# Exponentials in a pair of PSUM banks, scores through one bank by halves, three expert banks, three score copies and one E

## The chip, the cores and the metric

The kernel runs on one core of a Trainium2 chip. The metric is the device time of one execution in microseconds (us). The engines are PE (TensorE matmuls; PEld is its weight load), DVE (VectorE), ACT (ScalarE), POOL (GpSimd) and SP (SyncE, which issues the DMAs). SBUF is the working memory, PSUM the eight banks of 128 x 512 fp32 into which the matmuls write.

## The reference

Attention with a top-32 mask feeds two expert layers, all of it dense.

```python
scores = (1 / sqrt(D)) * q @ k.T                    # B=4, H=8, S=576, D=64
kth = 32nd largest score of each row
attn = softmax(where(scores >= kth, scores, -1e9))
x = (attn @ v) as (B*S, H*D)                        # 2304 tokens x 512
h = x @ w_in                                        # 512 x 2048
g = where(h >= 1, h, where(h <= -1, 0, (h + 1)**2 / 4))
x = g @ w_out                                       # 2048 x 512
out = (silu(x @ w_gate) * (x @ w_val)) @ w_out2     # 512 x 1536, 1536 x 512
```

The weights come as 64-bit floats. The kernel converts each of 68 blocks of 128 x 512 of them into a pair of fp32r tiles (high and low part), and a product is three fp32r passes.

## The kernel before, in words

**Planner.** The program first lists operations (`p.op(engine, planned duration, function, reads, writes, ...)`). A list scheduler (`Plan.schedule`) then lays them out forwards and backwards `ROUNDS` times with planned durations and a ring of buffers for each kind of tile, and keeps the shortest plan. The order in that plan is the program order of every engine, and engines run it strictly in order. A number such as `PORT` (added to the planned time of a conversion step) or `PS` only changes the order.

**Attention.** A unit is one batch b, one pair of heads hp and one block of query tiles: 256 queries (two tiles) or 320 (two and a half). A query tile has two heads (the half tile one), 144 tile-heads in all, 36 for each batch. Batch 0 runs "plain" (fp32 matmuls, lines 767 to 771), the others in fp32r passes (line 775). For each tile-head `qtile` does this: PE writes 128 x 576 scores into `pS`, a pair of PSUM banks (halves of 288 columns); ACT copies them to `C` in SBUF (L792); DVE finds the 32 largest by four rounds of MAX8 (L794) and three of MATCH_REPLACE8 (L804, into `R`); POOL makes the bias `nb` from the maximum (L798); ACT writes exp(scores) into `E` in SBUF (L801); and DVE applies the mask in place, reading `C` and `E` and writing `E` with the row sum (L808). PE then transposes `E` (L852 to L872), ACT takes the result out of the banks `pT` (L832, L837, L839), POOL makes low parts (L841). `outputs` multiplies by V (L696 plain, L707 and L709 otherwise), normalises and stores to `xs` in DRAM.

**Conversions.** `convert` makes one weight block: a DMA into `cv`, two ACT steps (L932, L935), a DVE step (L937), a POOL step (L940), ACT (L942), POOL (L944), and a DMA to scratch. With `bank` the DVE step reads one operand from a `pM` bank; without, both come from SBUF. The first `BANKED` = 24 conversions use a bank. The ten held ones come first, then 28 early ones, then 30 later ones inside the first two expert steps.

**Experts.** 2304 tokens run in groups of 256 (the last of 512) through fourteen steps, layer 1 or 2 of one or two groups each. `proj` (L1060) fills a `pM` bank with 24 matmuls of 256 columns or 12 of 512; layer 1 then takes it out by ACT Relu (L1136), ACT Square (L1138) and DVE min/max (L1140, which reads the bank again); layer 2 by ACT Tanh (L1196) and DVE (L1198, L1208). Second products are L1102 and L1174. There are four `pM` banks. After the attention the banks of `pS` and `pT` become expert banks too (named `late`). The first group's input is block 0 of batch 0, kept in SBUF; the second group's comes from block 1 of batch 0 through `xs`.

PSUM before: `pS` 2, `pT` 2, `pM` 4. SBUF rings that matter: `C` 2, `E` 2, `R` 2.

## Time and profile before

| | us |
|---|---|
| median of 3 runs (1304.3 to 1309.76) | 1307.21 |
| the profiled execution, whole time | 1309.97 |
| its span, first to last instruction | 1308.2 |
| PE busy (94% of the span) | 1225.9 |
| DVE busy (81%) | 1054.9 |
| ACT busy (69%) | 898.6 |
| POOL busy (60%) | 790.0 |

The difference of 1.8 us between the execution and its span lies around the first and last instruction. Busy shares are means over stages: attention lasts until about 1028 us, and after it only expert matmuls are left, so that DVE's 81% is a full engine for four fifths of the time. A matmul is counted busy from its start to its modelled end, so a busy PE has to be held against the pace of its matmuls.

### The profile page before, as it was taken

What the parts mean: (1) busy time and instruction counts of PE and PEld (TensorE: products, weight loads), DVE (VectorE), ACT (ScalarE), POOL (GpSimd) and SP (SyncE); (2) the same over time, 40 slices, a digit from 0 to 9 for tenths busy, and PEclk for the clock granted to TensorE, in tenths of its full rate; (3) what the DMA queues carried; (4) which work ended last, traced back from release to release, by engine and by line L of the source; (5) the groups of instructions that cost most, each with busy time, mean ns of one, the idle gap of its engine ahead of it and who ended that gap; (6) DMA issues with size and microseconds to landing.
All of it is one profiled execution on the core that took longest, in us unless ns stands there. A gap on an engine that the chain in (4) does not pass through costs nothing.

```text
span 1308.2 us, 23150 instructions
## 1 busy us (share of the span) xinstructions
PE 1225.9 (94%) x7744; PEld 1090.6 (83%) x7744; DVE 1054.9 (81%) x2070; ACT 898.6 (69%) x1921; POOL 790.0 (60%) x797
## 2 busy tenths in 40 slices
PE   3566799998999999999999999999999999999998
PEld 2444588886999999999999988889999888888887
DVE  6989999999999999999999999999999512222212
ACT  5767787678897788878989887779786421332220
POOL 4767778698886577857587774667654512213210
PEclk9967699999999999999999999999999999999999
DMA  7987799889998787877875844447768554666452
GB/s 214 346 251 261 264 325 327 323 284 317 350 332 311 255 321 271 300 263 252 321 253 208 307 136 152 148 171 282 288 241 301 194 201 163 231 226 231 154 193 65
DMA packets 145479, 328.16 MB, mean 251 GB/s; under 512 B 33616, under 2 KB 75088, under 8 KB 145360
## 3 DMA queue, kind: packets, MB, share of 16 engines
q1 hardware_dynamic: 145360, 326.69, 71.5%
q8 instruction: 61, 1.00, 0.3%
q14 instruction: 58, 0.48, 0.1%
HBM read 282.07 MB, written 44.56 MB: 250 GB/s over the span
## 4 chain that ended last, share of the span: by engine, by line
PE 68%; DMA 11%; DVE 10%; ACT 4%; issue 3%; POOL 3%; SPq 1%; POOLq 0%; DVEq 0%; ACTq 0%
PE pM L1060 27%; PE pM L1102 9%; PE pM L1174 8%; PE late L1060 5%; PE pS L775 4%; PE pT L707 4%; DVE v L794 4%; DVE R L804 3%; PE pT L852 3%; PE late L1174 2%; PE late L1102 2%; DMA cv<-in_moe_w_out_dram 2%; DMA ws_moe_w_out<-cv 2%; DMA cv<-in_moe_w_in_dram 1%; DVE E L808 1%
## 5 line engine op out<-in xcount | busy, mean ns | idle before, releaser
L794 DVE MAX8 v<-R 128x8 f32<-128x576 f32 x432 | 314.1, 746 | 0.9
L1060 PE MATMUL pM<-w,w 128*128 128x256 f32 (+1 forms) x1734 | 296.9, 314 | 3.2 <-DMA w<-ws_moe_w_in 1.9
L1060 PEld LDWEIGHTS pM<-w,w 128*128 128x128 f32 x1734 | 245.5, 192 | 22.7 <-DMA w<-ws_moe_w_in 2.6
L969 POOL TENSOR_TENSOR w<-t,w 128x512 fp32r<-128x512 f32 x106 | 142.4, 1346 | 189.4 <-ACT w L967 155.7
L841 POOL TENSOR_TENSOR late<-F,late 128x384 fp32r<-128x384 f32 (+1 forms) x180 | 179.4, 1008 | 61.9 <-ACT F L839 53.6
L804 DVE MATCH_REPLACE8 R<-v,R 128x576 f32<-128x576 f32 x288 | 212.6, 739 | 0.0
L808 DVE SCALAR_TENSOR_TENSOR E<-C,v,E 128x576 f32<-128x576 f32 x144 | 157.7, 1095 | 0.1
L1102 PE MATMUL pM<-w,w 128*128 128x256 f32 (+1 forms) x897 | 133.4, 292 | 0.0
L852 PE MATMUL pT<-idf,E 128*128 128x128 f32 x512 | 93.7, 292 | 41.3 <-DVE E L808 35.4
L792 ACT ACTIVATE C<-pS 128x576 f32<-128x576 f32 x144 | 94.0, 653 | 43.8 <-DVE E L808 37.7
L801 ACT ACTIVATE E<-C,nb 128x576 f32<-128x576 f32 x144 | 112.6, 783 | 15.4 <-POOL nb L798 14.7
L1102 PEld LDWEIGHTS pM<-w,w 128*128 128x128 f32 x897 | 117.7, 191 | 3.8 <-issue 1.5
L794 DVE MAX8 v<-C 128x8 f32<-128x576 f32 x144 | 107.4, 746 | 14.8 <-ACT C L792 13.8
L940 POOL TENSOR_TENSOR ct<-ct,cv 128x512 int32<-128x512 int32 x68 | 92.5, 1362 | 43.0 <-DVE cv L937 12.9
L852 PEld LDWEIGHTS pT<-idf,E 128*128 128x128 f32 x512 | 65.1, 148 | 58.1 <-DVE E L808 29.1
L967 ACT ACTIVATE w<-t 128x512 fp32r<-128x512 f32 x106 | 67.1, 635 | 59.2 <-DVE t L1208 52.6
L1060 PE MATMUL pM<-late,w 128*128 128x256 f32 (+1 forms) x618 | 107.4, 309 | 0.0
L804 DVE MATCH_REPLACE8 R<-v,C 128x576 f32<-128x576 f32 x144 | 106.5, 740 | 0.0
L837 ACT ACTIVATE late<-pT 128x384 fp32r<-128x384 f32 (+1 forms) x180 | 84.9, 472 | 14.2 <-PE pT L865 4.7
L1060 PEld LDWEIGHTS pM<-late,w 128*128 128x128 f32 x618 | 86.9, 190 | 4.9 <-POOL late L969 0.2
L1174 PE MATMUL pM<-w,w 128*128 128x512 f32 x324 | 88.8, 405 | 0.7 <-POOL w L944 0.6
L1060 PE MATMUL pM<-w,late 128*128 128x256 f32 (+1 forms) x456 | 86.1, 325 | 0.0
(151 smaller groups left out, 2661.3 us busy)
## 6 DMA issues: line engine op xcount, KB each, us to landing
w<-ws_moe_w_out SPq DMA_DIRECT2D x144, 512.0 KB, 5.9
w<-ws_moe_w_in SPq DMA_DIRECT2D x91, 512.0 KB, 6.3
w<-ws_moe_w_gate SPq DMA_DIRECT2D x56, 512.0 KB, 5.8
w<-ws_moe_w_val SPq DMA_DIRECT2D x51, 512.0 KB, 6.3
late<-ws_moe_w_out SPq DMA_DIRECT2D x40, 512.0 KB, 6.0
cv<-in_moe_w_out_dram SPq DMA_DIRECT2D x28, 512.0 KB, 5.2
late<-ws_moe_w_in SPq DMA_DIRECT2D x27, 512.0 KB, 6.5
cv<-in_moe_w_in_dram SPq DMA_DIRECT2D x16, 512.0 KB, 5.3
```

The lines of the kernel that those rows point to most:

```text
L792: p.op("ACT", self.act(576), lambda sc=sc, cc=cc: nc.scalar.activation(out=cc(), in_=sc(), func=AF.Copy), [ps], [Cb], 1, "scp")
L794: p.op("DVE", self.dve(576), lambda: nc.vector.max(out=v8[:, h, k, :], in_=rr() if k else cc()), [Rb if k else Cb], [(v8, (h, k))], 6, "max8")
L801: p.op("ACT", self.act(576, self.FN), lambda h=h, cc=cc, ee=ee: nc.scalar.activation(out=ee(), in_=cc(), func=AF.Exp, bias=nb[:, h:h + 1], ...
L804: p.op("DVE", self.dve(576) + 0.06, lambda h=h, k=k, cc=cc, rr=rr: nc.vector.match_replace(out=rr(), in_to_replace=v8[:, h, k, :], in_valu ...
L808: p.op("DVE", self.dve(576) + 0.06, lambda h=h, cc=cc, ee=ee: nc.vector.scalar_tensor_tensor(out=ee(), in0=cc(), scalar=v8[:, h, 3, 7:8], ...
L841: p.op("POOL", self.pool(n), lambda: nc.gpsimd.tensor_tensor(out=dst(1), in0=src(F), in1=dst(0).bitcast(F32), op=OP.subtract), [F, (PT, (0 ...
L852: fn = (lambda ps=ps, m=m, h=h, c=c: nc.tensor.transpose(ps[:, m * 128:(m + 1) * 128], Sb[:, h, 64 * h + c * 128:64 * h + (c + 1) * 128], ...
L940: p.op("POOL", self.pool(512), lambda: nc.gpsimd.tensor_tensor(out=ci(), in0=ci(), in1=word(0), op=OP.add), [(cv, 0)], [ct], 3, tag + "cvadd")
L969: p.op("POOL", self.pool(n), lambda: nc.gpsimd.tensor_tensor(out=dst[:, 1, to:to + n], in0=src[:, off:off + n], in1=dst[:, 0, to:to + n].b ...
L1060: nc.tensor.matmul(ps[:, at:at + n], W[:, w, k * 128:(k + 1) * 128], x[:, s, xat:xat + n], start=k == 0 and j == 0, stop=k == KC - 1 and j ...
L1102: nc.tensor.matmul(ps[:, at:at + n], WO[f][:, v, j * 128:(j + 1) * 128], g[:, s, gat:gat + n], start=q == 0 and m == 0, stop=q == 3 and m ...
L1174: nc.tensor.matmul(ps[:], a[:, s, at:at + 128], WO[f][:, v, :], start=q == 0 and m == 0, stop=q == 3 and m == 2)
```

## The change

Exponentials get their own ring `pE` of one pair of PSUM banks; ACT writes them there, and the mask reads them from there and writes `E` in SBUF. To pay for it, `pS` becomes one single bank, through which the two halves of a tile-head's scores pass one after the other, each with its own ACT copy of 288 columns; and `pM` goes from four banks to three. `C` goes from two buffers to three, `E` from two to one. `BANKED` goes to 40, which covers all 28 early conversions (14 of them before). `ROUNDS` goes from 4 to 10 and `PORT` from 0 to .38, which act on the order alone. The four zero fills of `vF` move out of the plan to the program's start.

```diff
-    ROUNDS = 4
+    ROUNDS = 10
...
-    VIA, BANKED = 0, 24
+    VIA, BANKED = 0, 40
...
+    PE_N, PM, PS_N, CN, EN, FB = 1, 3, 1, 3, 1, 2
...
-    SB, FN, PS, PORT = 0.043, 0.136, 0.065, 0.0
+    SB, FN, PS, PORT = 0.043, 0.136, 0.065, 0.38
...
-        self.r_E = R("E", [128, 2, S], F32, 2)
+        self.r_E = R("E", [128, 2, S], F32, self.EN)
...
-        self.p_s = R("pS", [128, 2, 512], F32, 1, "P")
-        self.r_C = R("C", [128, S], F32, 2)
+        self.p_s = R("pS", [128, 512], F32, self.PS_N, "P")
+        self.r_C = R("C", [128, S], F32, self.CN)
+        self.p_e = R("pE", [128, 2, 512], F32, self.PE_N, "P")
         self.p_t = R("pT", [128, 512], F32, self.PT_BANKS, "P")
-        self.p_m = R("pM", [128, 512], F32, 6 - self.PT_BANKS, "P")
+        self.p_m = R("pM", [128, 512], F32, self.PM, "P")
...
-        p.op("DVE", self.dve(1280), lambda: nc.vector.memset(vF[:], 0.0), [], [vF], 1, "vz")
...
-            ps = self.p_s.new()
             Rb = self.r_R.new()
+            Cb = self.r_C.new()
             for j in (0, 1):
+                ps = self.p_s.new()
...
+                p.op("ACT", self.act(288), lambda j=j, ps=ps, Cb=Cb: nc.scalar.activation(
+                    out=Cb[:, j * 288:(j + 1) * 288], in_=ps[:, 0:288], func=AF.Copy), [ps], [(Cb, j)], 1, "scp")
...
-            p.op("ACT", self.act(576), lambda sc=sc, cc=cc: nc.scalar.activation(out=cc(), in_=sc(), func=AF.Copy), [ps], [Cb], 1, "scp")
...
-            p.op("ACT", self.act(576, self.FN), lambda h=h, cc=cc, ee=ee: nc.scalar.activation(
-                out=ee(), in_=cc(), func=AF.Exp, bias=nb[:, h:h + 1], scale=0.125), [Cb, (nb, h)], [(Eb, h)], 1, "exp")
+            Ep = self.p_e.new()
+
+            def ep(Ep=Ep):
+                return Ep[:, :, 0:288]
+            p.op("ACT", self.act(576, self.FN), lambda h=h, cc=cc, ep=ep: nc.scalar.activation(
+                out=ep(), in_=cc(), func=AF.Exp, bias=nb[:, h:h + 1], scale=0.125), [Cb, (nb, h)], [Ep], 1, "exp")
...
-            p.op("DVE", self.dve(576) + 0.06, lambda h=h, cc=cc, ee=ee: nc.vector.scalar_tensor_tensor(
-                out=ee(), in0=cc(), scalar=v8[:, h, 3, 7:8], in1=ee(),
+            p.op("DVE", self.dve(576) + 0.06 + self.PS, lambda h=h, cc=cc, ee=ee, ep=ep: nc.vector.scalar_tensor_tensor(
+                out=ee(), in0=cc(), scalar=v8[:, h, 3, 7:8], in1=ep(),
                 op0=OP.is_ge, op1=OP.mult, accum_out=rs[:, i, h:h + 1]),
-                [Cb, (v8, (h, 3))], [(Eb, h), (rs, (i, h))], 5, "mask")
+                [Cb, Ep, (v8, (h, 3))], [(Eb, h), (rs, (i, h))], 5, "mask")
...
+        for r in self.r_vF:
+            nc.vector.memset(r.slots[0][:], 0.0)
```

What this does to the order is seen at three places. The first is DVE's order before, from the first mask to the second (a name's number tells the buffer: `C_283`, `C_284` are the two copies, `E_232` and `E_233` the two E).

```order
L808 SCALAR_TENSOR_TENSOR E_232,rs_243<-C_283,v_236,E_232 128x576
L937 SCALAR_TENSOR_TENSOR cv_278<-cv_278,pM_289 128x512
L804 MATCH_REPLACE R_235<-v_236,R_235 128x576
L937 SCALAR_TENSOR_TENSOR cv_279<-cv_279,pM_290 128x512
L794 MAX v_237<-C_283 128x8
L794 MAX v_236<-R_235 128x8
L804 MATCH_REPLACE R_234<-v_237,C_283 128x576
L808 SCALAR_TENSOR_TENSOR E_232,rs_243<-C_284,v_236,E_232 128x576
```

And the same stretch of DVE's order now, where line numbers are one to three off.

```order
L809 SCALAR_TENSOR_TENSOR E_232,rs_242<-C_282,v_235,pE_285 128x576
L791 MAX v_235<-R_234 128x8
L791 MAX v_236<-C_284 128x8
L805 MATCH_REPLACE R_234<-v_235,R_234 128x576
L805 MATCH_REPLACE R_233<-v_236,C_284 128x576
L938 SCALAR_TENSOR_TENSOR cv_277<-cv_277,pM_288 128x512
L791 MAX v_235<-R_234 128x8
L938 SCALAR_TENSOR_TENSOR cv_278<-cv_278,pM_289 128x512
L809 SCALAR_TENSOR_TENSOR E_232,rs_242<-C_283,v_235,pE_285 128x576
```

Both masks now read the one pair `pE_285`, so the exponential of the second stands between them; the third tile-head has a copy of its own (`C_284`), while before it had to wait for the first mask to give `C_283` back.

The second place is PE's order where the first expert step begins, before: a tile-head's scores (L769) go into the pair `pS_282` one after the other, and the experts rotate through four banks.

```order
L769 MATMUL pS_282<-kF_220,qF_228 128x64
L769 MATMUL pS_282<-kF_220,qF_228 128x224
L769 MATMUL pS_282<-kF_220,qF_228 128x288
L852 MATMUL pT_285<-idf,E_232 128x128 x2
L852 MATMUL pT_286<-idf,E_232 128x128 x2
L856 MATMUL pT_286<-idf,E_232 128x128
L769 MATMUL pS_282<-kF_220,qF_228 128x288
L1060 MATMUL pM_287<-w_265,w_254 128x256 x6
```

The same place of PE's order now.

```order
L1061 MATMUL pM_288<-w_264,w_253 128x256 x6
L1061 MATMUL pM_288<-w_263,w_255 128x256 x6
L1061 MATMUL pM_288<-w_264,w_255 128x256 x3
L770 MATMUL pS_281<-kF_220,qF_228 128x288
L1061 MATMUL pM_288<-w_264,w_255 128x256 x3
L1061 MATMUL pM_289<-w_264,w_257 128x256 x6
L1061 MATMUL pM_289<-w_263,w_259 128x256 x6
L1061 MATMUL pM_289<-w_264,w_259 128x256 x6
L770 MATMUL pS_281<-kF_221,qF_229 128x288
L1061 MATMUL pM_290<-w_264,w_261 128x256 x6
```

Between two halves of scores, which share `pS_281`, stand 21 expert matmuls, and the experts rotate through `pM_288` to `pM_290`.

The third place is DVE's order now, at the end of batch 1 (three masks near each other).

```order
L809 SCALAR_TENSOR_TENSOR E_232,rs_242<-C_282,v_237,pE_285 128x576
L805 MATCH_REPLACE R_234<-v_235,R_234 128x576
L791 MAX v_235<-R_234 128x8
L809 SCALAR_TENSOR_TENSOR E_232,rs_242<-C_283,v_237,pE_285 128x576
L791 MAX v_236<-C_282 128x8
L821 RECIPROCAL rc_245<-rs_242 128x4
L809 SCALAR_TENSOR_TENSOR E_232,rs_242<-C_284,v_235,pE_285 128x576
```

The last two masks have only a MAX8 and a reciprocal between them, and need the exponential pair and the one `E` in turn.

## Rows read from the trace of the kernel before

**Rows 1.** Four stretches: length, busy us of PE, PEld, DVE, ACT, POOL; clock, DMA share, GB/s.
```profile
0.00:160.00 160.00, 97.09 (x310) 64.83 (x310) 136.71 (x265) 111.10 (x214) 108.85 (x110) 0.80 0.83 269
160.00:331.00 171.00, 160.25 (x1030) 136.86 (x1030) 170.26 (x312) 138.32 (x281) 141.30 (x119) 0.98 0.90 312
331.00:1030.00 699.00, 694.50 (x5188) 661.84 (x5188) 687.43 (x1408) 577.68 (x1306) 475.74 (x519) 1.00 0.73 261
1030.00:1308.20 278.20, 274.04 (x1222) 227.03 (x1220) 60.53 (x88) 71.52 (x123) 64.11 (x51) 1.00 0.52 178
```

**Rows 2.** The chain that ended last: start, us, what; from two stretches.
```profile
413.84 6.11 PE pM L1060 x51
...
1040.17 10.91 PE pM L1060 x48
```

**Rows 3.** Timeline around the third expert step: start, us, engine, line, operation.
```profile
310.14 0.80 DVE L808 SCALAR_TENSOR_TENSOR E<-C,v,E 128x576 f32<-128x576 f32 x1
...
316.50 5.05 PE L696 MATMUL pT<-PF,vF 128*128 128x320 f32 x18
...
327.70 2.14 PE L1174 MATMUL pM<-w,w 128*128 128x512 f32 x8 [0.59 <-POOL w L944]
...
330.71 1.58 PE L1060 MATMUL pM<-w,w 128*128 128x256 f32 x12
```

**Rows 4.** The mask: ns min/median/max, first and last start us.
```profile
L808 DVE SCALAR_TENSOR_TENSOR E<-C,v,E x144: 789/942/1901, 27.8 to 1026.7; 128x576 f32<-128x576 f32 x144
```

**Rows 5.** DVE steps with and without a PSUM operand, as in rows 4.
```profile
L937 DVE SCALAR_TENSOR_TENSOR cv<-cv x44: 667/740/1865, 108.3 to 321.7; 128x512 int32<-128x512 int32 x44
L937 DVE SCALAR_TENSOR_TENSOR cv<-cv,pM x24: 666/687/699, 7.4 to 101.3; 128x512 int32<-128x512 int32 x24
L1140 DVE SCALAR_TENSOR_TENSOR t<-pM,t x66: 652/675/692, 168.3 to 1195.9; 128x512 f32<-128x512 f32 x66
```

**Rows 6.** Groups over the span: busy us, mean ns; idle us before them, releasers.
```profile
L808 DVE SCALAR_TENSOR_TENSOR E<-C,v,E 128x576 f32<-128x576 f32 x144 | 157.7, 1095 | 0.1
L794 DVE MAX8 v<-C 128x8 f32<-128x576 f32 x144 | 107.4, 746 | 14.8 <-ACT C L792 13.8 <-POOL nb L798 0.3 <-POOL late L503 0.3
L792 ACT ACTIVATE C<-pS 128x576 f32<-128x576 f32 x144 | 94.0, 653 | 43.8 <-DVE E L808 37.7 <-PE pS L775 2.0 <-PE pM L1060 1.5
L801 ACT ACTIVATE E<-C,nb 128x576 f32<-128x576 f32 x144 | 112.6, 783 | 15.4 <-POOL nb L798 14.7
L674 ACT ACTIVATE rb<-pT 128x256 f32<-128x256 f32 x32 | 12.2, 382 | 7.4 <-PE pT L668 6.7
```

**Rows 7.** DVE busy in the mask's line (two records a mask, which overlap).
```profile
0.00:160.00 160.00, 20.92 (x36) 0.80 0.83 269
160.00:331.00 171.00, 25.16 (x40) 0.98 0.90 312
331.00:1030.00 699.00, 112.81 (x212) 1.00 0.73 261
```

**Rows 8.** DVE's conversion step in two stretches.
```profile
L937 DVE SCALAR_TENSOR_TENSOR cv<-cv x14: 667/688/1103, 108.3 to 160.0; 128x512 int32<-128x512 int32 x14
...
160.00:331.00 171.00, 34.24 (x31) 0.98 0.90 312
```

**Rows 9.** What PE waited for after 331 us: us in total, times, longest.
```profile
PE pS L775 <- ACT C L792: 1.8, 2, 1.4
```

**Rows 10.** Timeline of ACT and DVE: one expert bank of layer 1.
```profile
621.49 0.70 ACT L1136 ACTIVATE t<-pM,one 128x512 f32<-128x512 f32 x1
...
625.00 1.27 DVE L1140 SCALAR_TENSOR_TENSOR t<-pM,t 128x512 f32<-128x512 f32 x2
```

**Rows 11.** Timeline: a POOL conversion step alone, and one while a mask runs.
```profile
142.24 1.29 POOL L940 TENSOR_TENSOR ct<-ct,cv 128x512 int32<-128x512 int32 x1 [2.09 <-DVE cv L937]
...
158.08 1.28 DVE L808 SCALAR_TENSOR_TENSOR E<-C,v,E 128x576 f32<-128x576 f32 x1
158.71 1.81 POOL L940 TENSOR_TENSOR ct<-ct,cv 128x512 int32<-128x512 int32 x1
```

More of the change, by code (lines that the diff above doesn't have):

```diff
@@ L412, in build @@
         self.r_PT = R("PT", [128, 2, 9, 320], F32R, 0)
-        self.r_F = R("F", [128, 512], F32, 2)
+        self.r_F = R("F", [128, 512], F32, self.FB)
         self.r_tmp = R("tmp", [128, 320], F32, 1)
@@ L437, in build @@
             p.heirs.append((gone, ring, n))
-        self.chain.append(((self.p_s, self.p_t), self.p_m, 2 + self.PT_BANKS))
+        self.chain.append(((self.p_s, self.p_e, self.p_t), self.p_m, 2 + self.PT_BANKS))
         p.heirs.append(self.chain[-1])
@@ L567, in prep_v32 @@
     def prep_v32(self, b, hp):
-        p, t = self.p, self.t["v"]
+        t = self.t["v"]
         vF = self.r_vF[hp].new()
-        nc = self.nc
-        p.op("DVE", self.dve(1280), lambda: nc.vector.memset(vF[:], 0.0), [], [vF], 1, "vz")
         for h in (0, 1):
@@ L760, in qtile, with mms, cc @@
                 rd = [qz, (kT, 0), (kT, 1), (kT, "a"), (kT, "b1")]
-            ps = self.p_s.new()
             Rb = self.r_R.new()
+            Cb = self.r_C.new()
             for j in (0, 1):
+                ps = self.p_s.new()
                 if plain:
-                    mine = [x for x in parts if x[0] == j]
+                    mine = [x[1:] for x in parts if x[0] == j]
                     def mms(ps=ps, mine=mine, r=r, cols=cols):
-                        for jj, at, a, z in mine:
-                            nc.tensor.matmul(ps[:, jj, at:at + z - a], q[r, cols], kT[r, 0, a:z], start=True, stop=True)
-                    p.op("PE", sum(self.mm(4 * (z - a)) for _, _, a, z in mine), mms, rd, [(ps, j)], 0, "qk")
-                    continue
-                def mms(j=j, ps=ps, lhs=lhs):
-                    for k, (l, hh, at) in enumerate(lhs):
-                        nc.tensor.matmul(ps[:, j, 0:288], l(), kT[:, hh, at + j * 288:at + (j + 1) * 288],
-                                         start=k == 0, stop=k == len(lhs) - 1)
-                p.op("PE", self.mm(288, len(lhs)), mms, rd, [(ps, j)], 0, "qk")
-            def sc(ps=ps):
-                return ps[:, :, 0:288]
+                        for at, a, z in mine:
+                            nc.tensor.matmul(ps[:, at:at + z - a], q[r, cols], kT[r, 0, a:z], start=True, stop=True)
+                    p.op("PE", sum(self.mm(4 * (z - a)) for _, a, z in mine), mms, rd, [ps], 0, "qk")
+                else:
+                    def mms(j=j, ps=ps, lhs=lhs):
+                        for k, (l, hh, at) in enumerate(lhs):
+                            nc.tensor.matmul(ps[:, 0:288], l(), kT[:, hh, at + j * 288:at + (j + 1) * 288],
+                                             start=k == 0, stop=k == len(lhs) - 1)
+                    p.op("PE", self.mm(288, len(lhs)), mms, rd, [ps], 0, "qk")
+                p.op("ACT", self.act(288), lambda j=j, ps=ps, Cb=Cb: nc.scalar.activation(
+                    out=Cb[:, j * 288:(j + 1) * 288], in_=ps[:, 0:288], func=AF.Copy), [ps], [(Cb, j)], 1, "scp")
+            def cc(Cb=Cb):
+                return Cb[:].rearrange("p (j n) -> p j n", j=2)
             def rr(Rb=Rb):
@@ L786, in ee @@
                 return Eb[:, h, :].rearrange("p (j n) -> p j n", j=2)
-            Cb = self.r_C.new()
-            def cc(Cb=Cb):
-                return Cb[:].rearrange("p (j n) -> p j n", j=2)
-            p.op("ACT", self.act(576), lambda sc=sc, cc=cc: nc.scalar.activation(out=cc(), in_=sc(), func=AF.Copy), [ps], [Cb], 1, "scp")
             def vmax(k, h=h, Cb=Cb, Rb=Rb, cc=cc, rr=rr):
```

## The prediction

> **What bounds the kernel now.** I read the busy time of four stretches first [rows 1]. From 331 us to the end PE is busy 694.5 of 699 us and 274.0 of 278.2, so 8.7 us idle in all; before 331 it idles 62.9 us of the first 160 and 10.8 of the next 171. DVE is the other full engine: 170.3 of 171 us and 687.4 of 699, until the attention ends.
>
> A busy PE may still be slow, so I hold it against its pace in the chain that ended last [rows 2]: 51 expert matmuls of 256 columns in 6.11 us are 120 ns each, 48 of 512 columns in 10.91 us are 227 ns. 256 and 512 columns at the granted 2.4 GHz level take 107 and 213 ns, so 13 ns is all that is lost per matmul. The change removes no matmul. After 331 us there is thus next to nothing to win on PE, however much DVE is relieved; what can be won lies ahead of 331.
>
> What happens at 331 is the third expert step, the first that needs the second block of batch 0 [rows 3]. The 36th mask, batch 0's last, starts at 310.14; the product with V follows at 316.50, and by way of DRAM the third step's first matmul comes at 330.71. For the 150 us ahead of that mask DVE had no gap. If DVE gets there earlier, everything behind slides forward. A second condition stands 3 us beside it: the last matmuls of the second step (L1174) wait until 327.70 for POOL to finish converted weights.
>
> **The mask.** It lasts 789 ns at best, 1095 in the mean and up to 1901 [rows 4, 6], on a fixed size. What its price is with one operand in PSUM, no row shows; the nearest are three steps on 512 columns [rows 5]. The conversion step with both operands in SBUF goes from 667 to 1865 ns, the same step with a PSUM operand from 666 to 699, and L1140, also with one, from 652 to 692. So the spread belongs to two SBUF operands, and the PSUM operand adds 687 - 667 = 20 ns at most. I take 789 + 20 = 809 ns. Bounds: 675 ns widened by 64 columns at 0.96 GHz, 742 ns, which has no row sum; and 1095, if the spread comes from something else than the second SBUF operand.
>
> At 809 the saving is .286 us a mask, 41 us over 144. Where it falls matters. In the mask's line [rows 7] the first 160 us hold 18 masks in 20.92 us, 1.16 each, the next stretch 20 in 25.16, 1.26 each, the rest 106 in 112.81, 1.06 each; the second record of a mask accounts for some .01 of each. So 18 x .345 = 6.2 us before 160, 18 x .44 = 7.9 from there to the 36th mask, and 26 us after 331, where PE does not care.
>
> Of the 7.9 I count all, since DVE is full. Of the 6.2 I count half, 3.1: DVE idles 23 us of the first 160 [rows 1], so other things also hold it. Bounds of both together: 0 and, at 742 ns, 16.5.
>
> One rule speaks for a smaller gain. The Trainium skill, Perfetto Trace Analysis, section Optimizing Scalar/DVE Operations, puts DVE's access overhead at about 60 ns on SBUF and 125 on PSUM; by that the mask would be 854 ns and the sum below smaller by 1.2 us. The 20 ns between the conversion steps [rows 5] do not bear out 65.
>
> **Banked conversions.** Fourteen more conversions read their operand from a bank. Those are the ones of 104 to 160 us, whose median is 688 ns without a bank [rows 8] against 687 with one [rows 5]: nothing. The thirty dear ones, 34.24 us for 31 rows after 160, 1.1 us each, stay as they are. Bounds 0 and 1.
>
> **The order** puts 62 conversion steps ahead of the 36th mask instead of 66. Four times 1.1 is 4.4 us, but the second step needs these weights too; I count 2 (0 to 4.4). It also puts ten more score matmuls and fifteen more transposes of batch 1, and six L1174 fewer, ahead of the third step: about 10 x .13 + 15 x .12 - 6 x .23 = 1.7 us of PE work, at the pace above, moved into the hole.
>
> **Scores by halves.** ACT's copy of 576 columns is 653 ns, an evacuation of 256 is 382 [rows 6]; between them 288 columns are .41, two halves .82, so .165 us more a tile-head, 24 us in all and 17.5 after 331. ACT goes there from 577.7 to 595 of 699 us [rows 1], 85%. That is no bound, but copies wait longer in its queue. The second half on PE waits for the first half's copy, and all expert matmuls behind it wait too. Cover is what stands between: 21 expert matmuls, 2.5 us, in the order shown. Uncovered it would cost .41 and two handoffs for each of 106 tile-heads, over 43 us. PE waited for a copy after 331 twice, 1.8 us in all [rows 9]; with twice as many handoffs I take 3.6, near that row, and 43 as the far end. The third copy helps: ACT idled 37.7 us until a mask gave a copy back [rows 6].
>
> **One exponential pair, one E.** The exponential of the next tile-head, 783 ns [rows 6], now waits for the last mask. At the first place shown seven DVE steps lie between two masks. At the third only a MAX8 of 746 and a reciprocal do, so DVE will stand there for the rest of the exponential and its handoffs. After 331 the 26 us that the masks give back pay for it; before, the order keeps masks apart. I cost it at 0; far end 13 us, .36 for each of the 36 masks of batch 0. The zero fills were at the program's start in DVE's order already: 0.
>
> **Three expert banks.** A bank of layer 1 is read from 621.49 (Relu) until DVE's min/max ends, near 625.64 [rows 10]: 4.15 us. A fill is 24 x .12 = 2.88 us, and with three banks PE returns after two other fills, 5.75 us, earlier if nothing stands between. It fits with 1.6 us to spare, so 0, and DVE is quicker than before. Far end below.
>
> **Sum.** -3.1 - 7.9 - 2 - 1.7 + 3.6 = -11.1. The execution profiled took 1309.97, so 1298.9; the median of the runs is 2.8 lower, so I forecast 1296.
>
> **Rivals.**
>
> Larger gain. POOL's conversion step takes 1.29 us alone and 1.81 beside a mask [rows 11]. POOL and DVE keep each other out, and with the mask's operand in PSUM POOL is freed as well: up to 38 masks x .52 = 20 us of its 250 busy us before 331 [rows 1]. If conversions set the pace there, half of it is on the path: 10 us more, 1286, and with the whole 6.2 us of the start 1283. Against it: DVE, not POOL, was without a gap. The Trainium skill, SBUF — State Buffer, section Who interferes with whom, has the rule: a DVE instruction with two SBUF inputs and a GpSimd one that reads SBUF lock each other out, whichever starts first. The rows on the mask and on POOL agree.
>
> No change. Conversions end when their transfers allow. DMA engines are busy .90 of the stretch from 160 to 331 at 312 GB/s [rows 1]. If converted weights still come at 328, the second step ends where it did, and only the 3 us between it and the third can go: 1304. For it speaks that 327.70 is so near 330.71; against it that each conversion passes through DVE's queue and gets nearer to the front there.
>
> Slower. The hold of 4.15 us becomes longer than the 5.75 us in which PE returns, since ACT's queue is longer by the half copies; PE then stalls at each fill of the saturated stretch. It decides from 1.6 us of extra delay in ACT and DVE together. Some 50 of L1140's 66 fills lie there; .5 us each is 25 us: 1321.
>
> Nothing is done: excluded, the order shows the mask reading `pE`.
>
> **Chances.** The forecast (1288 to 1304) 0.47, larger gain 0.15, no change 0.22, slower 0.16. Half a per cent, 6.5 us, is what a measurement tells from nothing, so faster means below 1300.7. Four fifths of the forecast's share lie there: .38 + .15 gives 0.53 faster; 0.30 same, of which .08 from the forecast; 0.17 slower with the upper edge of no change. The range reaches to 1277 below (the larger gain with the mask at 742) and to 1317 above, most of the way to the slower case.
>
> **What would show it.** The mask near 810 ns with almost no spread; the 36th mask about 11 us earlier, near 299; the third step's first matmul near 318 to 320; PE without new idle time after it; attention over earlier, DVE with gaps after 331. I am wrong if PE waits show the copies or L1140's bank after 331, if L1174 of the second step still waits for POOL near 328, or if the first 160 us get longer because PE, granted 0.80 of its clock there [rows 1], serves the halves more slowly.

## The result, and the profile after

| | before | after |
|---|---|---|
| median of the runs, us | 1307.57 (10 runs, 1304.3 to 1309.76) | 1313.1 (10 runs, 1311.65 to 1319.9) |
| the profiled execution: whole, span, us | 1309.97, 1308.2 | 1311.65, 1309.6 |

The ratio is 1.0052, 95% interval 1.0035 to 1.0069: the changed kernel is slower by 5.5 us. The forecast was 1296, on the other side. The time lies inside the stated range only because that was stretched toward the slower rival, whose mechanism did not come.

First the part that came as forecast. The line of the mask in the changed kernel (duration in ns, least, median, greatest, then the first and last start):

```profile
L809 DVE SCALAR_TENSOR_TENSOR E<-C,v,pE x144: 791/803/817, 26.1 to 1017.5; 128x576 f32<-128x576 f32 x144
```

and the same line by stretches:

```profile
0.00:160.00 160.00, 13.78 (x34) 0.79 0.81 269
160.00:331.00 171.00, 17.79 (x44) 0.99 0.86 303
331.00:1030.00 699.00, 85.35 (x210) 1.00 0.73 261
```

Against [rows 4, 7] the spread of 789 to 1901 ns is gone, and the masks take 116.9 us instead of 158.9. DVE's busy time over the whole span fell by the same amount, from 1054.9 to 1013.0 us. The conversion steps without a bank kept their spread [rows 8]:

```profile
L938 DVE SCALAR_TENSOR_TENSOR cv<-cv x30: 672/1046/1784, 165.4 to 328.2; 128x512 int32<-128x512 int32 x30
```

So 42 us of the engine that had no gap were freed, and the time did not fall. Where they went is seen in the four stretches of the changed kernel, with the columns of [rows 1], and in the one row that holds everything ahead of 340 us:

```profile
0.00:160.00 160.00, 99.12 (x292) 59.04 (x293) 132.34 (x269) 111.20 (x231) 101.94 (x111) 0.79 0.81 269
160.00:331.00 171.00, 160.47 (x1037) 134.98 (x1036) 163.99 (x318) 142.14 (x308) 130.67 (x118) 0.99 0.86 303
331.00:1030.00 699.00, 695.77 (x5205) 664.46 (x5205) 654.79 (x1395) 581.56 (x1411) 450.37 (x521) 1.00 0.73 261
1030.00:1308.20 278.20, 275.43 (x1216) 227.78 (x1214) 61.91 (x90) 69.39 (x116) 62.26 (x50) 1.00 0.51 182
...
0.00:340.00 340.00, 267.94 (x1372) 201.10 (x1372) 303.75 (x603) 261.15 (x558) 241.26 (x236) 0.89 0.84 289
```

and the same long row of the kernel before:

```profile
0.00:340.00 340.00, 265.39 (x1401) 209.33 (x1402) 315.90 (x592) 256.72 (x511) 259.15 (x237) 0.89 0.87 293
```

Ahead of 340 us DVE is busy 303.75 instead of 315.90 us: 12.15 us less, near the 14.1 that the sum had from the masks (6.2 + 7.9). But PE has done 1372 matmuls by then instead of 1401, in more busy time. By shape 42 expert matmuls of 256 columns and 6 of 512 are missing, 6.4 us at the pace of the prediction, against 19 smaller ones more, some 2.3 us. DVE's gain became idle time of DVE. From 160 to 331 PE is busy 160.47 us, before it was 160.25: it idles 10.5 instead of 10.8 us. The second stretch had little idle time of PE for the forecast's gain to begin with.

Two waits show what DVE stands for instead. DVE's waits from 0 to 160 us after (total us, times, longest):

```profile
DVE cv L938 <- ACT pM L933: 16.8, 15, 2.6
DVE E L809 <- ACT pE L802: 2.5, 1, 2.5
```

and before:

```profile
DVE cv L937 <- ACT pM L932: 10.6, 11, 2.2
DVE v L794 <- ACT C L792: 6.1, 3, 3.0
```

The conversions with a bank wait for ACT to fill it: 6.2 us more, against 4.4 us less of DVE's busy time in this stretch.

PE's own waits changed most. Over the whole span, nearly all of it ahead of 160 us, after:

```profile
PE pS L770 <- ACT C L778: 33.6, 23, 4.7
PE pT L853 <- DVE E L809: 12.8, 6, 5.4
```

and before:

```profile
PE pT L852 <- DVE E L808: 35.4, 16, 6.5
PE pS L769 <- ACT C L792: 8.1, 8, 1.8
```

PE waits 22.6 us less for masked exponentials to transpose, and 25.5 us more for ACT to copy batch 0's scores out of their bank. The 176 matmuls that make these scores are also busy longer (busy us and mean ns, then the idle time of PE before them; the ends are modelled); before and after:

```profile
L769 PE MATMUL pS<-kF,qF 64*128 64x288 f32 (+3 forms) x176 | 64.0, 501 | 9.5 <-ACT C L792 8.1 <-ACT qF L592 1.3
L770 PE MATMUL pS<-kF,qF 64*128 64x288 f32 (+3 forms) x176 | 74.0, 526 | 35.5 <-ACT C L778 33.6
```

So the quicker masks did spare PE waits, and the halves of batch 0 took as much: the one bank has to be emptied before the second half can go in.

The marks of the forecast, read from the first or last start on a line: the 36th mask starts at 300.4 us (before 310.1, forecast near 299). The last conversion step, though, starts at 328.2 (before 321.7), the second step's matmuls end at 342.2 (330.9), and the third step starts at 337.1 (330.7; forecast 318 to 320). Around it, PE's timeline of the changed kernel (start, us, instruction, in brackets the idle time before it):

```profile
327.75 0.53 PE L775 MATMUL pS<-late,late 128*128 128x288 f32 x2 [1.03 <-ACT C L778]
329.76 2.93 PE L1175 MATMUL pM<-w,w 128*128 128x512 f32 x6 [1.48 <-ACT big L978]
...
333.49 2.24 PE L1175 MATMUL pM<-w,w 128*128 128x512 f32 x9
...
336.38 0.85 PE L1175 MATMUL pM<-w,w 128*128 128x512 f32 x3
337.07 0.64 PE L1061 MATMUL pM<-w,w 128*128 128x256 f32 x4
```

Where [rows 3] had the last matmuls of the second step at 327.70, nine of them now start at 333.49, and more follow after 340. The late second step is near what the prediction named as a sign of being wrong, but the wait seen there is for ACT's `big`, 1.48 us, and none for POOL from 315 to 345 us. After 331 us things came as forecast: PE's waits there for a score copy are small.

```profile
PE pS L775 <- ACT C L778: 1.7, 3, 0.7
```

PE even idles less from 331 to 1030, 3.2 instead of 4.5 us, and has by 1030 made up for the number of matmuls it was behind (1372 + 5161 and 1401 + 5125 by the windows from 340 on). The number mixes sizes, though: from 1030 to 1308.2 PE is still busy 275.43 us for 1216 matmuls, before 274.04 for 1222 [rows 1].

### The profile page after: what moved, and what is told of

Read it like the earlier page. It is cut to its first block, busy times and chain, and to the rows that moved or that the text cites. A ratio compares the mean times of both kernels' runs of the same rounds, so it can differ in the third digit from the quotient of the medians.

```text
span 1309.6 us, 23261 instructions
## 1 busy us (share of the span) xinstructions
PE 1230.8 (94%) x7744; PEld 1086.3 (83%) x7744; DVE 1013.0 (77%) x2070; ACT 904.3 (69%) x2065; POOL 745.2 (57%) x797
## 4 chain that ended last, share of the span: by engine, by line
PE 82%; DMA 5%; POOL 2%; ACT 1%; issue 1%; SPq 0%; DVE 0%; ACTq 0%; POOLq 0%; DVEq 0%
PE pM L1061 30%; PE pM L1103 14%; PE late L1061 8%; PE pM L1175 8%; PE pS L775 5%; PE pT L707 4%; PE pT L853 3%; PE late L1175 2%; PE pS L770 2%; PE pT L696 2%; PE late L1103 1%; DMA w<-ws_moe_w_out 1%; PE pT L709 1%; DMA cv<-in_moe_w_val_dram 1%; DMA ws_moe_w_gate<-cv 1%
## 5 line engine op out<-in xcount | busy, mean ns | idle before, releaser
L1061 PE MATMUL pM<-w,w 128*128 128x256 f32 (+1 forms) x1905 | 317.4, 311 | 2.8 <-DMA w<-ws_moe_w_in 2.6
L1061 PEld LDWEIGHTS pM<-w,w 128*128 128x128 f32 x1905 | 265.2, 190 | 22.0 <-issue 4.0
L842 POOL TENSOR_TENSOR late<-F,late 128x384 fp32r<-128x384 f32 (+1 forms) x180 | 168.0, 945 | 76.1 <-ACT F L840 70.1
L1103 PE MATMUL pM<-w,w 128*128 128x256 f32 (+1 forms) x873 | 142.7, 297 | 0.3 <-DMA w<-ws_moe_w_out 0.3
L778 ACT ACTIVATE C<-pS 128x288 f32<-128x288 f32 x288 | 121.5, 422 | 27.2 <-PE pS L775 17.5
L809 DVE SCALAR_TENSOR_TENSOR E<-C,v,pE 128x576 f32<-128x576 f32 x144 | 115.8, 804 | 21.3 <-PE pT L857 11.0
L1103 PEld LDWEIGHTS pM<-w,w 128*128 128x128 f32 x873 | 120.4, 191 | 6.2 <-issue 2.2
L941 POOL TENSOR_TENSOR ct<-ct,cv 128x512 int32<-128x512 int32 x68 | 89.9, 1324 | 46.6 <-ACT ct L936 23.9
L968 ACT ACTIVATE w<-t 128x512 fp32r<-128x512 f32 x116 | 75.2, 652 | 58.3 <-DVE t L1209 52.4
L802 ACT ACTIVATE pE<-C,nb 128x576 f32<-128x576 f32 x144 | 108.8, 755 | 4.8 <-DVE E L809 4.0
L770 PE MATMUL pS<-kF,qF 64*128 64x288 f32 (+3 forms) x176 | 74.0, 526 | 35.5 <-ACT C L778 33.6
L775 PE MATMUL pS<-late,late 128*128 128x288 f32 x384 | 85.5, 304 | 4.5 <-ACT C L778 4.5
L840 ACT ACTIVATE F<-pT 128x384 f32<-128x384 f32 (+1 forms) x180 | 85.7, 480 | 1.3 <-POOL late L842 0.8
```

The lines of the kernel that those rows point to most:

```text
L775: nc.tensor.matmul(ps[:, 0:288], l(), kT[:, hh, at + j * 288:at + (j + 1) * 288], start=k == 0, stop=k == len(lhs) - 1)
L778: p.op("ACT", self.act(288), lambda j=j, ps=ps, Cb=Cb: nc.scalar.activation(out=Cb[:, j * 288:(j + 1) * 288], in_=ps[:, 0:288], func=AF.Co ...
L802: p.op("ACT", self.act(576, self.FN), lambda h=h, cc=cc, ep=ep: nc.scalar.activation(out=ep(), in_=cc(), func=AF.Exp, bias=nb[:, h:h + 1], ...
L809: p.op("DVE", self.dve(576) + 0.06 + self.PS, lambda h=h, cc=cc, ee=ee, ep=ep: nc.vector.scalar_tensor_tensor(out=ee(), in0=cc(), scalar=v ...
L842: p.op("POOL", self.pool(n), lambda: nc.gpsimd.tensor_tensor(out=dst(1), in0=src(F), in1=dst(0).bitcast(F32), op=OP.subtract), [F, (PT, (0 ...
L1061: nc.tensor.matmul(ps[:, at:at + n], W[:, w, k * 128:(k + 1) * 128], x[:, s, xat:xat + n], start=k == 0 and j == 0, stop=k == KC - 1 and j ...
```

## The experiments

The theories. **Conversions**: the start of the third step sets the time, and weights that are converted late hold it. **New waits**: what the banks were paid with (halves, three banks, one E) costs the time. **Order**: the three constants cost it (ROUNDS and PORT act on the order alone; BANKED also takes 14 more conversions through a bank). Later came **Transfers** (DMA sets the pace of conversions), **Engines** (ACT, DVE and POOL set it), **Clock** (the loss is a lower granted clock) and **Idle** (the loss is idle time of PE). The runs are given by question. "Steps ahead" is the number of the 68 conversion steps that stand ahead of the 36th mask in DVE's order. All times in us.

| run | time, ratio to before [95%] | steps ahead | last conversion | 36th mask | third step |
|---|---|---|---|---|---|
| before | 1307.6 | 66 | 321.7 | 310.1 | 330.7 |
| after | 1313.1, 1.0052 [1.0035, 1.0069] | 62 | 328.2 | 300.4 | 337.1 |
| e1_order | 1312.9, 1.0043 [1.0027, 1.0059] | 65 | 323.6 | 311.4 | 329.4 |
| e5_after_old | 1321.6, 1.0112 [1.0098, 1.0126] | 57 | 337.5 | 289.2 | 344.0 |
| e6_banked40 | 1320.2, 1.0097 [1.0083, 1.0111] | 59 | 328.8 | 293.1 | 344.9 |
| e7_port38 | 1313.4, 1.0046 [1.0032, 1.0060] | 66 | 316.2 | 313.2 | 330.9 |
| e4_halves | 1357.6, 1.0372 [1.0341, 1.0404] | 68 | 316.6 | 318.4 | 335.7 |
| e2_light0 | 1307.1, 0.9999 [0.9989, 1.0008] | 55 | 342.4 | 254.5 | 354.1 |
| e3_cv5 | 1320.8, 1.0099 [1.0075, 1.0124] | 66 | 327.1 | 318.2 | 338.9 |
| e8_half_stores | 1299.0, 0.9943 [0.9930, 0.9955] | 62 | 319.5 | 291.6 | 327.1 |
| e9_port08 | 1325.3, 1.0143 [1.0123, 1.0163] | 67 | 331.7 | 330.2 | 333.9 |
| e10_port12 | 1334.1, 1.0225 [1.0203, 1.0246] | 68 | 337.6 | 338.9 | 320.3 |
| e11_early10 | 1314.0, 1.0055 [1.0039, 1.0071] | 68 | 310.7 | 311.6 | 325.4 |
| e12_before_port12 | 1351.0, 1.0345 [1.0323, 1.0366] | 67 | 351.6 | 350.1 | 341.4 |
| e15_after_early12 | 1306.4, 0.9976 [0.9965, 0.9987] | 65 | 318.9 | 306.6 | 324.5 |
| e16_before_early12 | 1316.6, 1.0060 [1.0043, 1.0077] | 65 | 322.4 | 307.9 | 332.1 |

### Is it the constants or the structure? (e1, e5, e6, e7)

e1: the kernel before with the three constants of the change.

```diff
-    ROUNDS = 4
+    ROUNDS = 10
-    VIA, BANKED = 0, 24
+    VIA, BANKED = 0, 40
-    SB, FN, PS, PORT = 0.043, 0.136, 0.065, 0.0
+    SB, FN, PS, PORT = 0.043, 0.136, 0.065, 0.38
```

> The kernel before with only the constants of the order changed (ROUNDS 10, PORT .38, BANKED 40). Three theories on why the change gained nothing. Conversions: the weight conversions set the pace until the second expert step has its weights (the 38th conversion step of DVE was at 160.0 us before and at 158.7 after the change, the last at 321.7 and 328.2), so that DVE time saved in masks becomes waiting. New waits: the saving is on the path, but score halves, one E and one exponential pair take it back. Order: the constants put conversions behind masks, and the second expert step ends later. If order is the cause, this kernel is slower than before by what the change was, 4 to 7 us (1311 to 1315), with the last conversion step near 328. If conversions or new waits are, it stays within 3 us of 1307.6.

The three constants alone bring a loss of the same size, 5.3 us, with pS, pM, C and E as they were. Held against this run, which has the same constants, the rest of the change is worth nothing: 1312.9 and 1313.1. So the next runs took them apart, from both kernels. e5: the changed kernel with the old constants.

```diff
-    ROUNDS = 10
+    ROUNDS = 4
-    VIA, BANKED = 0, 40
+    VIA, BANKED = 0, 24
-    SB, FN, PS, PORT = 0.043, 0.136, 0.065, 0.38
+    SB, FN, PS, PORT = 0.043, 0.136, 0.065, 0.0
```

> The change with the old constants (ROUNDS 4, PORT 0, BANKED 24), so the pair of banks, the halves, three copies and three expert banks alone. By order, 57 instead of 62 conversion steps now stand ahead of the 36th mask. Adding: the constants alone cost 5.3 us in the kernel before, so without them the change is at 1313.1 - 5.3 = 1308, no slower than before. Conversions: what sets the start is how many conversion steps stand behind the masks, so with five more behind it the third step starts later than 337 and the time is 1313 to 1320.

e6: the kernel before with one of them.

```diff
-    VIA, BANKED = 0, 24
+    VIA, BANKED = 0, 40
```

> The kernel before with BANKED 40 alone. By order, 59 instead of 66 conversion steps stand ahead of the 36th mask. Conversions: the second step ends later than 331, the time is slower than before by about what ROUNDS, PORT and BANKED together cost (5 us, 1313) or more. Dear operands: conversions of 104 to 160 us gain nothing from a bank but the bank and ACT's handoff tie them to PE, so also slower, with the loss ahead of 160 us: conversion 38 later than 160.0. Neither: 1307 to 1308.

e7: the kernel before with another.

```diff
-    SB, FN, PS, PORT = 0.043, 0.136, 0.065, 0.0
+    SB, FN, PS, PORT = 0.043, 0.136, 0.065, 0.38
```

> The kernel before with PORT .38 alone; 66 conversion steps stand ahead of the 36th mask, as before. Conversions: nothing was moved behind the masks, so 1307 to 1309. If the loss of the three constants together comes from PORT in another way, 1312 to 1314.

ROUNDS was not tried by itself. Adding is refuted: without the constants the changed kernel is 8.5 us slower still, so they cost the kernel before 5.3 us and are worth 8.5 to the changed one. Conversions fits e5 and e6 (fewer steps ahead, third step at 344 to 345, 13 to 14 us lost) and not e7, where nothing is moved behind a mask, the third step starts where it did, and 6 us are lost all the same. Dear operands, tied in e6 to a 38th conversion step later than 160.0, is refuted there: it starts at 156.6.

### What do halves cost by themselves? (e4)

The kernel before with the scores by halves through one bank, and the second bank left unused; C stays at two buffers.

```diff
-        self.p_s = R("pS", [128, 2, 512], F32, 1, "P")
+        self.p_s = R("pS", [128, 512], F32, 1, "P")
...
+                p.op("ACT", self.act(288), lambda j=j, ps=ps, Cb=Cb: nc.scalar.activation(
+                    out=Cb[:, j * 288:(j + 1) * 288], in_=ps[:, 0:288], func=AF.Copy), [ps], [(Cb, j)], 1, "scp")
...
-            p.op("ACT", self.act(576), lambda sc=sc, cc=cc: nc.scalar.activation(out=cc(), in_=sc(), func=AF.Copy), [ps], [Cb], 1, "scp")
```

> The kernel before with scores by halves through one bank, and nothing else (two copies C, two E, four expert banks, exponential in SBUF). New waits: DVE now waits for copies, 18 us or more over the attention, and the time is 1318 to 1345. Conversions: the halves cost little ahead of 331 us and PE has room after it, 1307 to 1312.

50 us slower, the largest effect of all. DVE's waits from 331 to 1030 us in e4:

```profile
DVE v L790 <- ACT C L778: 33.7, 46, 3.0
```

and in the changed kernel:

```profile
DVE E L809 <- PE pT L857: 10.6, 14, 2.1
DVE t L1199 <- ACT t L1197: 8.3, 4, 5.9
DVE v L791 <- ACT C L778: 5.9, 9, 1.9
```

DVE stands for a copy 46 times (13 times, 7.3 us, before). The reading, argued: the first half's copy needs a free buffer of C, and only after it can PE write the second half. With the rest of the change that wait is down to 5.9 us; the rest holds the third copy, but the copy was not tried apart from it. So the price of halves was real, far above the 3.6 us that the sum had as a wait of PE, and after 331 us the change pays it off itself. Ahead of that it does not. In e4, with nothing of the change but the halves, batch 0's score matmuls show the same shift as in the change, 28.5 us of waits for copies instead of 8.1 and 72.1 us busy instead of 64.0:

```profile
L770 PE MATMUL pS<-kF,qF 64*128 64x288 f32 (+3 forms) x176 | 72.1, 514 | 30.0 <-ACT C L778 28.5
```

### Is it DVE's time? (e2) The transfers? (e3, e8)

e2: the changed kernel with one selection round less in batch 0, so that its rows keep 24 instead of 32 scores. MAX8 and MATCH_REPLACE of 36 tile-heads are left out, .75 and .74 us each, 54 us of DVE's work.

```diff
-            for k in range(3):
+            last = 2 if plain else 3
+            for k in range(last):
...
```

> The changed kernel with one selection round fewer in batch 0 (its rows keep 24 scores, not 32). This takes a MAX8 (.748 us) and a MATCH_REPLACE8 (.742 us) from each of 36 tile-heads, 54 us of DVE ahead of the third expert step. Conversions: 36th mask 30 to 50 us earlier, but first and second expert step hardly move and the time is 1306 to 1313. New waits (DVE's queue decides): the third expert step starts 20 us or more earlier and the time is below 1293.

The 36th mask starts at 254.5, 46 us earlier than with the change, and the time falls by 6 us, to that of the kernel before. PE's row from 160 to 331 us points at the reason:

```profile
160.00:331.00 171.00, 160.07 (x1063) 139.07 (x1061) 152.55 (x285) 148.60 (x331) 137.82 (x127) 0.95 0.87 301
```

DVE now has 18 us of gaps there, and PE is busy 160.07, as ever. The prediction counted DVE's time ahead of 331 as time of the program because DVE had no gap. This run takes 46 us away from the way to that mark and gets 6. That refutes the step, with one reserve: the run also got an order of its own (55 steps ahead), and what that costs is not parted from it. In the first 160 us it did help PE, which idles 43.2 instead of 60.9 us there. But over the whole span PE then idles 12.7 us less (66.1 instead of 78.8) and is busy 11.8 us longer (1242.6 instead of 1230.8) for the same 7744 matmuls. The granted clock from 160 to 331 is .95 instead of .99, which can be a part of that; the rest is open. The run also refutes the mark: the third step starts at 354.1, later than in any other run, with the time of the kernel before.

e3: a fifth buffer for conversions, paid for with one of the 15 weight buffers.

```diff
-    NW, GR, TR, BIG, CV, CT, QT, HELD = 15, 6, 5, 2, 4, 2, 1, (6, 4)
+    NW, GR, TR, BIG, CV, CT, QT, HELD = 14, 6, 5, 2, 5, 2, 1, (6, 4)
```

> The changed kernel with five buffers cv for conversions in flight, not four, paid for by one weight buffer (14, not 15). Conversions: the 38th conversion step comes 8 to 20 us earlier than 158.7, the last 5 to 15 earlier than 328.2, and the time falls by 4 to 12 us, 1301 to 1309. New waits or order: conversions come earlier without any gain, 1311 to 1316.

The 38th conversion step comes at 150.7 instead of 158.7, and the kernel is slower by 7.7 us than the change. Early conversions alone are no gain; whether the missing weight buffer or the order makes the loss was not separated.

e8: each conversion stores half of its block, and later loads read that half twice; the engines' order stays.

```diff
-        self.dma(lambda: W[:].rearrange("p s n -> p (s n)").bitcast(F32), lambda: scr[:], 512 * 1024,
+        self.dma(lambda: W[:].bitcast(F32), lambda: scr[:, None, 0:512].to_broadcast([128, 2, 512]), 512 * 1024,
...
-        self.dma(lambda: scr[:], flat, 512 * 1024, reads=[W], writes=[self.xdeps[key]], prio=6, tag="stw")
+        self.dma(lambda: scr[:, 0:512], lambda: flat()[:, 0:512], 512 * 1024, reads=[W], writes=[self.xdeps[key]], prio=6, tag="stw")
```

> The change, but each conversion stores only half of its block to scratch, and later loads read that half twice; the order of all engines stays the same and the output is not the reference's. Of what DMA moves ahead of 331 us, 68 half blocks of 256 KB are gone. Transfers: if conversions end when their transfers allow, the last conversion step comes 10 us or more ahead of 328, the third step ahead of 330, and the time falls to 1305 or less. Engines: if ACT, DVE and POOL in their order set the pace of conversions, the last conversion stays within 3 us of 328 and the time at 1311 to 1314.

The fastest run, 14 us ahead of the change. Its windows:

```profile
0.00:160.00 160.00, 108.81 (x356) 67.40 (x356) 139.91 (x285) 118.58 (x248) 110.08 (x119) 0.81 0.72 226
160.00:331.00 171.00, 161.59 (x1023) 136.13 (x1023) 164.21 (x320) 141.88 (x313) 131.22 (x120) 0.97 0.79 263
```

What the trace shows of it lies ahead of 160 us: PE has done 356 matmuls there instead of 292, DVE is busy 139.9 instead of 132.3 us, and the first expert step starts 10 us earlier (its first matmul at 141.7 instead of 151.8). After that the 30 conversions of the first two steps take 170.6 us, as with the change (169.5), though DMA's share is down from .86 to .79. So Transfers is right ahead of 160 and Engines after it. Of PE's 60.9 idle us of the first stretch 9.7 went with half of the stores. That is less than with DVE's work in e2 (17.7), so DVE and the transfers both hold that stretch. SP's own waits there, in the changed kernel, are the link, since a buffer is loaded again only when its store has landed (the longest, for POOL, is no transfer):

```profile
SPq L387 <- POOL cv L945: 21.7, 16, 2.1
SPq L387 <- DMA ws_moe_w_out<-cv: 16.5, 9, 5.3
SPq L387 <- DMA ws_moe_w_gate<-cv: 8.6, 4, 3.3
SPq L387 <- DMA ws_moe_w_in<-cv: 7.9, 6, 3.1
```

### Is it the conversions behind the masks? (e9 to e12)

Three runs set the changed kernel's order so that 67 or 68 conversion steps stand ahead of the 36th mask, by a higher planned price of a conversion step (e9, e10) or by fewer conversions ahead of the first expert step (e11, which also leaves 30 conversions with a bank, not 38). The fourth, e12, gives e10's price to the kernel before.

```diff
-    SB, FN, PS, PORT = 0.043, 0.136, 0.065, 0.38
+    SB, FN, PS, PORT = 0.043, 0.136, 0.065, 0.8
```

> The change with PORT .8 instead of .38, which acts on the order alone: 67 conversion steps stand ahead of the 36th mask instead of 62. Conversions: the second step ends near 330 instead of 342, the hole in PE and the fall of the granted clock at 320 to 340 get shorter, and of the 14 us between old and new constants (57 and 62 steps ahead: 1321.6 and 1313.1) the next five steps give back as much again: 1303 to 1308. Price alone: if the order of conversions does not matter, 1313.

```diff
-    SB, FN, PS, PORT = 0.043, 0.136, 0.065, 0.38
+    SB, FN, PS, PORT = 0.043, 0.136, 0.065, 1.2
```

> The change with PORT 1.2: all 68 conversion steps stand ahead of the 36th mask. Conversions: as with .8 or 1 to 2 us better, 1302 to 1307, second step ended by 330, 36th mask later than 305. Overshoot: masks held back make the third step late through the product with V, and the time turns up again, 1308 or more, with the last product with V after 325.

```diff
-    PRE, EARLY = 3, (14, 14)
+    PRE, EARLY = 3, (10, 10)
```

> The change with EARLY (10, 10) instead of (14, 14): eight conversions fewer ahead of the first expert step, the eight more inside the first two steps; all 68 conversion steps stand ahead of the 36th mask. Conversions: what counts is that none stands behind the masks, so 1302 to 1308 and the first step starts earlier than 163.5. Early ones: if conversions ahead of the first step are what feeds PE, the first two steps wait for weights and the time is 1315 or more.

```diff
-    SB, FN, PS, PORT = 0.043, 0.136, 0.065, 0.0
+    SB, FN, PS, PORT = 0.043, 0.136, 0.065, 1.2
```

> The kernel before with PORT 1.2: 67 conversion steps ahead of the 36th mask instead of 66. With PORT .38 it took 1313.4 at 66. Conversions: there is nothing left to bring forward, so 1307 to 1313. If a high price helps whatever it moves, 1304 or less.

Here Conversions fell. With all of them ahead, e10 starts the third step at 320.3, earlier than any kernel here and where the prediction wanted it, and takes 1334 us. DVE's first two waits from 160 to 340 us in e10 and its row up to 331:

```profile
DVE cv L938 <- ACT cv L933: 18.1, 12, 3.1
DVE t L1141 <- ACT t L1139: 6.6, 4, 2.2
```

```profile
160.00:331.00 171.00, 154.82 (x957) 129.56 (x958) 131.31 (x256) 122.17 (x258) 120.77 (x108) 0.95 0.85 301
```

The conversion steps stand in DVE's order ahead of their own operands and wait 18 us for ACT, and the masks stand behind them: DVE is busy 131 of 171 us, the 36th mask starts 38 us later than in the change, and PE has 957 matmuls done instead of 1037. e11 starts its first step at 123.3 (18 matmuls, the rest from 153.9 on; the change has 6 before 160), its third at 325.4, 12 us ahead of the change, and takes the same time: PE has 357 matmuls done at 160 us, the change 292, but 1382 and 1372 at 340, so the lead is gone by then. e12 loses 45 us with the dial that cost e10 21.

### Where do the 5.5 us lie? (e13 to e16)

e13 and e14 are the two kernels once more, for a second pair of traces.

> The changed kernel once more, unchanged, for a second trace and its time beside the next run. The first pair of traces differs by 1.4 us, the medians by 5.6. Clock: if what is missing is the granted clock ahead of 160 us, this trace has a mean clock of .79 or less there against .80 or more in the trace of the kernel before, and a span of 1311 or more. Idle: if PE waits, its idle time over the whole span is 3 us or more above the other's.

> The kernel before once more, unchanged, for a second trace: 1307 by its median, span 1305.5. Clock: its share of time at the upper level ahead of 331 us is above that of the changed kernel by about 4 us. Idle: PE idles 3 us less than in the changed kernel.

Medians 1314.1 and 1309.9, against 1309.4 for the other runs of the kernel before on that chip: ratios 1.0038 [1.0024, 1.0052] and 0.9998 [0.9987, 1.0008]. The traces repeat themselves: the milestones of the table come within 2 us of those of the first pair. By 340 us the kernel before has done 1404 matmuls, the changed one 1367:

```profile
0.00:340.00 340.00, 266.50 (x1404) 210.33 (x1405) 316.17 (x593) 258.10 (x511) 261.16 (x237) 0.89 0.87 293
```

```profile
0.00:340.00 340.00, 267.38 (x1367) 200.48 (x1367) 303.64 (x602) 260.61 (x557) 239.50 (x235) 0.88 0.84 288
```

The loss ahead of 340 us is thus in both pairs, 29 and 37 matmuls, and most of it is there at 160 us: 310 and 309 matmuls done before, 292 and 285 after. Some of it comes back after 340. But the second pair of spans differs by 2.0 us (1308.5 and 1310.5), the first by 1.4, and the medians by 4.2 and 5.5. Clock was wrong in its size (mean granted clock ahead of 160: .78 and .79), and Idle in its sign: over the whole span the changed kernel's PE idles 79.5 us, that of the kernel before 81.5 (78.8 and 82.3 in the first pair). What the traces place is therefore busy time: PE is busy 4.0 and 4.9 us longer for the same 7744 matmuls, and the score matmuls of batch 0 alone are busy 10 us longer in both pairs. Between 2 and 4 us of the difference show in no trace. Which execution was profiled is part of it: in the first pair the kernel before is 2.4 us above its median and the change 1.5 below.

e15 and e16 give both kernels a value of EARLY between those tried. In e15 that also leaves 34 conversions with a bank, not 38.

```diff
-    PRE, EARLY = 3, (14, 14)
+    PRE, EARLY = 3, (12, 12)
```

> The change with EARLY (12, 12): four conversions fewer ahead of the first expert step. Transfers: what DMA must move ahead of the first step sets its start; (10, 10) brought it from 163.5 to 153.9, so (12, 12) brings it to 158 to 160. PE's idle time: what is won there is lost again between 200 and 340 us, as with (10, 10), so 1311 to 1315. A middle way that wins: 1308 or less.

> The kernel before with EARLY (12, 12). Transfers: its first expert step starts at 157 to 159 instead of 161.6. PE's idle time: lost again by 340 us, 1306 to 1311. A middle way that wins: 1303 or less, and better than both kernels.

The same edit makes the changed kernel 7.7 us faster (1314.1 to 1306.4) and the kernel before 6.6 slower (1309.9 to 1316.6). e15 beats both kernels, the one before by 0.24%, its interval clear of 1. Its windows:

```profile
0.00:160.00 160.00, 103.97 (x310) 62.50 (x310) 132.62 (x268) 112.87 (x236) 104.09 (x112) 0.79 0.82 270
0.00:340.00 340.00, 273.53 (x1411) 206.21 (x1412) 301.58 (x597) 261.54 (x557) 247.86 (x239) 0.89 0.85 292
340.00:1030.00 690.00, 686.22 (x5137) 655.04 (x5136) 651.70 (x1386) 575.50 (x1395) 437.34 (x511) 1.00 0.72 256
```

PE has 310 matmuls done at 160 us, as many as the kernel before, and 1411 at 340, where the change has 1372, with DVE no less idle than in the change. It did not come quite as Transfers had it: the first expert step does start earlier, at 136.9 instead of 151.8, but with 18 matmuls ahead of 160 us, and the bulk of it comes from 164.6 on. What differs is what PE was given to do; why that is better is not shown.

## Why the prediction was wrong

**The mask.** Right: 809 ns forecast, 803 in the median, and 42 us in all against 41. The rule of the Trainium skill (Perfetto Trace Analysis, section Optimizing Scalar/DVE Operations) made it 854 ns, an estimate; the least of 791 against 789 in SBUF [rows 4] shows 2 ns of extra price where the rule has 65.

**The gain ahead of 331.** This is the step that failed, in two places; a third is the next paragraph. "Of the 7.9 I count all, since DVE is full": DVE's 36th mask did come 10 us earlier, but e2, with 54 us less of DVE's work, shows that most of this time was not the program's. A full DVE had PE beside it that was full too, 160 of 171 us, and PE's 10.8 idle us of the stretch are not the wait for DVE: they stay between 8 and 13 in every run here but e10 and e12, which have 16 to 17. And "if DVE gets there earlier, everything behind slides forward" took a mark for the end: in e2 the third step starts 23 us later than before at the same time, in e10 ten earlier at 28 us more, in e11 five earlier at 7 us more. PE does attention work in the place of expert work; the order in which they come moves the mark, and not the sum of PE's work.

**Halves ahead of 331.** The sum has 3.6 us for PE's waits for copies after 331 and, without a reason, nothing ahead of it. There the price fell due: 25.5 us more of PE's waits for copies, and batch 0's score matmuls 10 us longer busy. e4 has both with the halves alone. The 22.6 us that PE waits less for masks were spent on this, and PE has 292 matmuls done at 160 us instead of 310. The prediction's last sign, PE serving the halves more slowly in the first 160 us, is thus the one that came, as waits above all. How much of the 5.5 us this makes no run shows: e5, with the same halves, has 307 matmuls done at 160 us.

**The start.** The 3.1 us of it: DVE's busy time there did fall, by 4.4 us, and 6.2 us of waits for ACT's banks took its place. The 14 more banked conversions do not explain them: in e6, which has these too, that wait is 10.4 us, as before (10.6). What lengthens it is open. e8 shows that the stores bound that stretch beside DVE.

**The order.** Counted as a gain of 2 + 1.7; the sign was wrong. With four more conversion steps behind the last mask of batch 0, PE has 29 matmuls fewer done by 340 us, and e7, where PORT changes nothing but the order, loses 6 us in the kernel before. Over one constant, EARLY at (10, 10), (12, 12), (14, 14), the changed kernel takes 1314.0, 1306.4, 1313.1: an order is worth some 8 us, most of the whole sum (in the changed kernel the constant also moves a few conversions off their banks; in the kernel before it does not, and costs 6.6).

**Halves after 331.** 3.6 forecast as an added wait, 1.7 measured where 1.8 was before: nothing was added. The far end of 43 us was real too: e4 has 50, as waits of DVE for copies, and not of PE for a bank as the far end was argued.

**One exponential pair, one E; three expert banks.** Costed at 0, and PE loses nothing there after 331. The masks do wait for PE's transposes, 10.6 us from 331 to 1030 in the waits above, paid from what they gave back.

**The rivals.** No change was the nearest: the second step does end late, with a few us on top; but late conversions as the cause fell with e10 and e11. Larger gain: POOL is freed, 745 instead of 790 us busy, its step L940 is 1324 instead of 1362 ns in the mean, and nothing came of it. Slower by the banks did not happen.

**Open.** That PE's gain from the masks went to the halves of batch 0 is seen in the traces and in e4; what makes the change 5.5 us slower, and not equal, is not shown by an experiment. The traces place 1.4 and 2.0 us of the difference, the medians are 4.2 to 5.5 us apart. Which property of an order makes it good is not found: neither the conversions ahead of the 36th mask nor any of the marks goes with the time over these runs; nearest is how much of PE's work is done by 340 us, and that only for like kernels.

## What to carry to other kernels

Where two engines are full side by side, time taken from the one cannot be counted as the program's: here PE had 10.8 idle us beside DVE, and nothing came of it (argued from e2, in one kernel). A price has to be asked for in each stretch: the halves were priced where PE was full, and cost where it was waiting. Before a mark inside the program is used for its end, a cheap run that moves the mark (leaving out work on its path, as in e2) shows whether the end goes with it. When the order comes from a scheduler, an edit has to be compared with both orders of its neighbourhood: the same structure was 0.5% slower or 0.2% faster by one constant.

## What was not expected of the hardware

The mask lasts 791 to 817 ns with one operand in PSUM, beside a POOL as busy as it is; the least is within 2 ns of the best with both operands in SBUF [rows 4].

After a hole in PE's work the granted clock falls, and PE pays for the hole a second time. In e10, rows of 10 us around the end of the second step (the third number from the right is the granted clock):

```profile
320.00:330.00 10.00, 6.61 (x34) 5.13 (x32) 10.00 (x21) 6.08 (x15) 6.91 (x8) 0.83 0.66 236
330.00:340.00 10.00, 6.93 (x25) 5.40 (x26) 8.02 (x17) 8.52 (x20) 7.25 (x7) 0.61 0.34 113
```

PE is busy 6.6 of the first ten and the clock of the next ten is .61 in the mean, most of it at 1.2 GHz. In the changed kernel the same place shows .98 and .85, with PE busy 6.2 and 9.3 of the ten.
